# A gated convolution and MLP kernel on one core: one convolution over all tokens, or two causal halves with the second beside the first half's MLP

## The chip, the core and the metric

The kernel runs on one core of one Trainium2 chip. The core has a matrix engine (PE, with PEld for its weight loads), a vector engine (DVE), an activation engine (ACT), a small general engine (POOL) and a queue engine (SP) that issues most DMA transfers. PE writes into PSUM, eight banks of 512 f32 values per partition; only DVE and ACT read PSUM here. The metric is device time in microseconds; lower is better.

## What is computed

Two layers, each with a mixer A and an MLP B, on x of 2048 tokens and 512 channels. The reference, cut to what matters:

```
def _A_ref(q, k, v, shift_k, ssm_k, ssm_D):
    k_shift = sum of 4 taps of k along the tokens, per channel
    kv = k_shift * v
    y = causal convolution of kv with ssm_k (2048 taps per channel, by FFT of length 2 * S)
    y = y + kv * ssm_D
    return q * y

def _B_ref(x, w1, b1, w2, b2):
    h = gelu(layernorm(x) @ w1 + b1)          # 512 -> 1376
    return h @ w2 + b2                        # 1376 -> 512

x = A_q
x = x + _A_ref(_layernorm(x), A_k, A_v, ...)
x = x + _B_ref(_layernorm(x), ...)
x = x + _A_ref(_layernorm(x), A_k, A_v, ...)
x = x + _B_ref(_layernorm(x), ...)
```

The inner branch of A depends only on k, v and the filters, so y is the same in both layers and is computed once. It has no dependence on x: the convolution must be there before the first product with q, and nothing else.

## The kernel before

Everything is bf16 in one SBUF tensor (`ar`), with f32 statistics in `sm` and one PSUM tensor (`ps`). The program first records operations with their reads and writes (`P.op`), then orders them, then adds waits, then emits one instruction stream per engine. An engine executes its stream in order.

**The convolution** is a transform over half-integer frequencies of length 4096, done by matmuls. A token is t = 16 b + a, with b on the 128 partitions.
- `turn`-like code (L749) transposes the filter on PE into that layout; the result is evicted by L664 or L663 (the helper `evac`: DVE copies with `tensor_copy`, ACT with `activation`, either may take it).
- `stage1` (L757, matmul at L766): 64 columns of data as weights, 128 columns of cosines or sines; real and imaginary parts go to the two halves of the PSUM partitions. 256 matmuls for the filter, 256 for kv.
- `stage2` (L772, L779) for the filter, with 128 columns, and the same in `products` (L861, L872) for kv, with 64 columns. The weights are a 4 MB table that SP loads in 16 pieces.
- `products` multiplies by the filter's transform with two operands at once (L658 through the helper `tt`, 128x2048): the filter's transform R_H and a copy R_HS with real and imaginary partitions exchanged. The copy is made by 16 SBUF-to-SBUF DMAs of 256 KB.
- `inverse1` (L884, L896), 256 matmuls of 128 columns, and `inverse2` (L938, L953), 64 matmuls of 256 columns.
All of it is done in two channel parts, `PARTS`.

**The shift filter** (4 taps): two of four channel blocks of 128 go through PE (`shift_pe`, L802: transposes at L810, matmuls with diagonal tap matrices at L827, the product with v at L834), two on DVE (`shift_tt`, L837: seven operations of 128x2048 and one product per block, L658).

**The MLP part** is a loop over two layers and blocks of tokens (16 token tiles of 128): `BLOCKS0 = (1,1,2,2,2,2,2,2,2)` and `BLOCKS1 = (4,4,4,4)`. Per block: statistics on DVE (L985, L987), reciprocal root on POOL (L991, L993), normalisation on DVE (L1000), x += norm * y (two L658), statistics and normalisation again, a transposition (PE at L1047 for the first two tiles, a DMA on SP for the others), m1 (L1060: 44 matmuls with the block's tokens as columns), gelu on ACT (L1065), m2 (L1093: 11 matmuls of 512 columns per token tile; the last tile in three pieces at L1082), and the residual sum on DVE (L1097).

**The order** comes from a list scheduler in `schedule`: each operation has a cost, a priority (its path to the end plus table entries in BIAS and PB), an earliest time (HOLD), and PSUM banks from pools. DMAs are issued in program order on SP. In that order all of the convolution stands ahead of the MLP, which begins when `inverse2` has delivered its first token tiles.

Of the kernel before, what the change touches and what calls it, by code (L numbers as in the profile page):

```python
# [22 lines left out]
class Pool:  # L23


    def __init__(self, nb, cap, gate=False):
        self.nb, self.cap, self.used, self.gate = nb, cap, 0, gate


class Tile:  # L30


    def __init__(self, pool):
        self.pool = pool
        self.base = None
        self.left = 0
        self.ops = []


class Op:  # L40
    __slots__ = ("i", "engs", "eng", "fn", "dur", "preds", "succ", "prio", "tile", "dma", "start", "end",
                 "pos", "inc", "waits", "val", "npred", "ready", "bytes", "base", "extra", "gate", "tag", "allow")


class Prog:
# [6 lines left out]
    BIAS = {'': 1044190, 'fir0': 816272, 'fir1': 594035, 'fir2': 1000293455, 'fir3': 475782, 'h1': 868926, 'h2': 42492, 'ht': 880650, 'i1_0': 1240071, 'i1_64':  # L52
# [6 lines left out]
    SHY = {'fir0': 1021, 'fir1': 277, 'h1': 55, 'h2': 0, 'ht': 0, 'i1_0': 0, 'i1_64': 365, 'i2_0': 61, 'i2_64': 0, 'x1_0': 0, 'x1_1': 8, 'x1_2': 1351, 'x1_3':  # L59
        1268, 'x2_0': 0, 'x2_64': 462, 'z0': 261, 'z1': 833}  # L60
    PB = {0: 150814, 1: -52106, 2: -225577, 3: -123331, 4: 999221868, 9: 1276405, 44: 1379512, 45: 1434690, 47: 506509, 49: 453148, 51: 999588645, 52:
# [131 lines left out]
    def __init__(self, nc):  # L193
        self.nc = nc
        self.ops = []
        self.state = {}
        self.nodes = [(-1, None)]
        self.cache = {}
        self.tag = ""


    def _cells(self, ap):
# [59 lines left out]
    def op(self, eng, fn, dur, reads=(), writes=(), tile=None, dma=None, prio=0.0, nbytes=0, gate=()):  # L262
# [11 lines left out]
        for t in o.tile:  # L274
            for p in t.ops:
                preds.add((p.i, "psum"))
            t.ops.append(o)
            t.left += 1
# [14 lines left out]
    def _place(self, tiles, s):  # L293

        got, taken = [], set()
        for t in tiles:
# [4 lines left out]
            for b in range(0, 8, pool.nb):  # L301
# [4 lines left out]
                if best is None or k < best:  # L306
                    best = k
# [826 lines left out]
```

## Time and profile before

| what | value |
|---|---|
| median of 3 runs | 242.58 us (241.78 to 242.68) |
| span of the profiled execution | 239.8 us |
| what lies around the span, by the median | 2.8 us |
| PE busy / share / instructions | 226.5 us, 94%, 2310 |
| DVE | 175.7 us, 73%, 363 |
| ACT | 142.9 us, 60%, 223 |
| POOL | 34.8 us, 15%, 75 |
| DMA | 27.40 MB, mean 114 GB/s |
| granted PE clock, mean | 1.000 |
| first L1060 matmul (m1), last L1082 matmul (m2) | 84.2 us, 237.5 us |

The span runs from the first to the last instruction of the profiled execution; the page has no total time for that execution, so its span is compared with the median of the runs, which also holds the launch and the end. A matmul's duration on the page contains its latency, so that neighbours overlap and the sum of durations is more than the time in which PE was occupied. Prices per instruction are therefore better taken from runs of like instructions in the timeline or the chain: the run's length by its count. "Idle before" is the time an engine had nothing, with the event that ended it.

### The profile page before, as it was taken

What the parts mean: (1) busy time and instruction counts of PE and PEld (TensorE: products, weight loads), DVE (VectorE), ACT (ScalarE), POOL (GpSimd) and SP (SyncE); (2) the same over time, 40 slices, a digit from 0 to 9 for tenths busy, and PEclk for the clock granted to TensorE, in tenths of its full rate; (3) what the DMA queues carried; (4) which work ended last, traced back from release to release, by engine and by line L of the source; (5) the groups of instructions that cost most, each with busy time, mean ns of one, the idle gap of its engine ahead of it and who ended that gap; (6) DMA issues with size and microseconds to landing.
All of it is one profiled execution on the core that took longest, in us unless ns stands there. A gap on an engine that the chain in (4) does not pass through costs nothing.

```text
span 239.8 us, 5559 instructions
## 1 busy us (share of the span) xinstructions
PE 226.5 (94%) x2310; PEld 151.5 (63%) x2330; DVE 175.7 (73%) x363; ACT 142.9 (60%) x223; POOL 34.8 (15%) x75
## 2 busy tenths in 40 slices
PE   7988899886899999999999999999999999999996
PEld 3876777775899885777767665754444444444453
DVE  0779999999997989989999996978997401211214
ACT  3697999999998994665556253464532552436200
POOL 3250000000012222223141032022130100000000
PEclk9999999999999999999999999999999999999999
DMA  6999999999910004222020203313022203210022
GB/s 231 338 387 385 384 235 272 249 282 337 375 63 0 3 0 48 45 44 48 0 44 5 42 1 68 66 23 68 0 44 44 87 3 69 62 44 0 3 98 77
DMA packets 37035, 27.40 MB, mean 114 GB/s; under 512 B 19506, under 2 KB 29969, under 8 KB 37010
## 3 DMA queue, kind: packets, MB, share of 16 engines
q1 hardware_dynamic: 36446, 26.91, 38.1%
q8 instruction: 18, 0.29, 0.5%
q10 hardware_dynamic: 564, 0.14, 0.4%
q14 instruction: 7, 0.06, 0.1%
HBM read 16.82 MB, written 2.10 MB: 79 GB/s over the span
## 4 chain that ended last, share of the span: by engine, by line
PE 71%; DVE 15%; DMA 4%; ACT 4%; SPq 3%; issue 2%; DVEq 0%
PE ps L1060 32%; PE ps L1093 30%; DVE ar L658 8%; PE ps L896 5%; DMA ar<-in_A_v_dram 4%; ACT ar L663 4%; DVE ar L664 4%; SPq L647 3%; DVE ar L834 2%; PE ps L1082 1%; PE ps L872 1%; DVE sm L985 1%; PE ps L953 1%; DVE ar L1000 0%; PE ps L766 0%
## 5 line engine op out<-in xcount | busy, mean ns | idle before, releaser
L1065 ACT ACTIVATE ar<-ps,sm 128x256 bf16<-128x256 f32 (+5 forms) x143 | 67.8, 522 | 72.8 <-PE ps L1060 70.1
L1060 PE MATMUL ps<-ar 128*128 128x256 bf16 (+5 forms) x568 | 83.7, 296 | 0.2
L1093 PE MATMUL ps<-ar 128*128 128x512 bf16 (+1 forms) x329 | 78.9, 379 | 0.7
L663 ACT ACTIVATE ar<-ps 128x1024 bf16<-128x1024 f32 (+2 forms) x79 | 73.9, 1055 | 8.0 <-PE ps L766 3.2
L1060 PEld LDWEIGHTS ps<-ar 128*128 128x128 bf16 (+1 forms) x572 | 53.2, 100 | 29.4 <-ACT ar L1065 0.4
L658 DVE TENSOR_TENSOR ar<-ar 128x512 bf16<-128x512 bf16 (+3 forms) x108 | 63.8, 628 | 1.8 <-DMA ar<-in_A_k_dram 1.4
L1093 PEld LDWEIGHTS ps<-ar 128*128 128x128 bf16 (+1 forms) x341 | 33.2, 98 | 34.5
L1097 DVE TENSOR_TENSOR ar<-ar,ps 128x512 bf16<-128x512 bf16 x31 | 20.8, 682 | 43.2 <-PE ps L1093 43.1
L985 DVE BATCH_NORM_STATS2 sm<-ar 128x6 f32<-128x512 bf16 (+1 forms) x68 | 42.6, 650 | 0.3
L1000 DVE TENSOR_SCALAR ar<-ar,sm 128x512 bf16<-128x512 bf16 x64 | 24.1, 401 | 6.6 <-POOL sm L993 6.3
L993 POOL TENSOR_TENSOR sm<-sm 128x2 f32<-128x2 f32 (+2 forms) x26 | 20.5, 787 | 2.2
L766 PE MATMUL ps<-ar 128*64 128x128 bf16 x512 | 17.6, 221 | 3.0 <-DVE ar L664 1.0
L991 POOL TENSOR_SCALAR sm<-sm 128x2 f32<-128x2 f32 (+2 forms) x26 | 5.9, 226 | 95.9 <-DVE sm L987 95.7
L766 PEld LDWEIGHTS ps<-ar 128*64 128x64 bf16 x512 | 14.9, 110 | 5.4 <-DVE ar L664 1.3
L664 DVE CAST ar<-ps 128x1024 bf16<-128x1024 f32 (+1 forms) x15 | 17.5, 1181 | 0.4 <-PE ps L872 0.2
L896 PE MATMUL ps<-ar 128*128 128x128 bf16 x256 | 15.1, 220 | 1.0 <-DVE ar L658 0.5
L896 PEld LDWEIGHTS ps<-ar 128*128 128x128 bf16 x256 | 14.5, 114 | 1.4 <-ACT ar L663 0.8
L872 PE MATMUL ps<-ar 128*128 128x64 bf16 x256 | 9.6, 193 | 2.3 <-ACT ar L663 2.1
L664 DVE COPY ar<-ps 128x2048 bf16<-128x2048 bf16 (+1 forms) x6 | 5.7, 954 | 7.6 <-PE ps L749 7.4
L987 DVE BATCH_NORM_AGGREGATE sm<-sm 128x2 f32<-128x6 f32 (+1 forms) x64 | 10.8, 177 | 0.6
L872 PEld LDWEIGHTS ps<-ar 128*128 128x128 bf16 x256 | 8.2, 98 | 3.5 <-ACT ar L663 3.4
L779 PE MATMUL ps<-ar 128*128 128x128 bf16 x128 | 8.7, 220 | 0.9 <-ACT ar L663 0.8
(33 smaller groups left out, 72.0 us busy)
## 6 DMA issues: line engine op xcount, KB each, us to landing
ar<-tab_s SPq DMA_DIRECT2D x16, 256.0 KB, 10.0
ar<-ar SPq DMA_DIRECT2D x16, 256.0 KB, 4.6
ar<-in_A_ssm_k_dram SPq DMA_DIRECT2D x4, 512.0 KB, 5.5
ar<-in_A_k_dram SPq DMA_DIRECT2D x8, 256.0 KB, 7.7
ar<-in_A_v_dram SPq DMA_DIRECT2D x8, 256.0 KB, 9.7
ar<-in_A_q_dram SPq DMA_DIRECT2D x4, 512.0 KB, 7.8
out_dram<-ar SPq DMA_DIRECT2D x7, 256.0 KB, 2.0
ar<-in_B_w_dram SPq DMA_DIRECT2D x1, 1376.0 KB, 12.0
```

What stands on the lines that cost most here:

```text
L658: return P.op(eng, lambda e: e.tensor_tensor(o, a, b, op), dur, reads=[a, b] + list(more), writes=[o])
L663: return e.activation(dst, src(), AF.Copy)
L664: return e.tensor_copy(dst, src())
L766: r = e.matmul(Q(tl, 64 * ri, 64, i * 128, [1, 128]), w, m, start=True, stop=True)
L896: r = e.matmul(Q(tl, 0, 128, i * 128, [1, 128]), w, m, start=q == 0, stop=q == 1)
L985: P.op(DVE, lambda e, sj=sj, x=x: e.bn_stats(sj, x), 40.0 + 1.1 * w, reads=[x], writes=[sj], gate=gate)
L993: P.op(POOL, lambda e: e.tensor_tensor(r, v, hf, ALU.pow), 430.0 + 150.0 * n, reads=[v, hf], writes=[r])
L1000: P.op(DVE, lambda e: e.tensor_scalar(o, x, m, r, ALU.subtract, ALU.mult), 335.0, reads=[x, m, r], writes=[o])
L1060: r = e.matmul(Q(tl, 0, rows, 0, [1, w]), a, m, start=dk == 0, stop=dk == 3)
L1065: P.op(ACT, lambda e, dst=dst, tl=tl, rows=rows, bias=bias, w=w: e.activation(dst, Q(tl, 0, rows, 0, [1, w]), AF.Gelu_apprx_tanh, bias=bia ...
L1093: r = e.matmul(Q(tl, 0, 128, 0, [1, 512]), ins[fc][0], ins[fc][1], start=fc == 0, stop=fc == 10)
L1097: P.op(DVE, lambda e, x=x, tl=tl: e.tensor_tensor(x, x, Q(tl, 0, 128, 0, [1, 512]), ALU.add), 640.0, reads=[x], writes=[x], tile=tl)
```

## The change

The convolution is cut into two causal halves of 1024 tokens. With h0 and h1 the halves of the filter and X0 and X1 the transforms of the halves of kv, a transform of length 1024 over half-integer frequencies gives the lower half of a product as its real part and the upper half as its imaginary part. So the first half of y is the real part of H0 X0, and the second half is the real part of H0 X1 + (H1 - i H0) X0. Only the even frequencies of the former transform are needed (`k1 = 2 * arange`), and a token is now t = 8 b + a within a half.

- Stage 1 and stage 2 are done for h0, kv0, h1 and kv1. Stage 2 has 16 matmuls of 64 columns per tile, in all four cases, and writes its output in PSUM in groups of 4 columns.
- For the second half, `h2_1` forms H1 - i H0 as it leaves PSUM (16 `scalar_tensor_tensor` on DVE), a second set of eight swap DMAs exchanges its partitions, `p2` multiplies with X0 (8 operations of 2048), and `x2_1` has a product and a sum (8 of each) before the second `inverse1`.
- `inverse2` has 32 matmuls of 512 columns.
- The shift filter of all four channel blocks runs on PE, per half, with matmuls of 64 rows that use the two halves of the partitions and write to two banks. Keys of the first half are transposed on PE, those of the second by eight DMA transposes on SP.
- The first half's MLP (both layers, `BLOCKS` (1,1,2,2,2) and (2,2,2,2)) is interleaved with the second half's convolution; the second half's MLP, with blocks of 4, follows.
- The normalisation may run on DVE or ACT; for ACT, POOL computes minus mean times scale (two more operations per block).
- The list scheduler is gone. `arrange` takes a written order of all 1200 operations (SEQ), a letter for the engine of each operation that has a choice (ENGS) and a PSUM bank for each tile (BANKS).

The diff, cut to its core:

```
-    k1 = np.arange(128)[None, :]
+    k1 = 2 * np.arange(128)[None, :]
...
-PE_CH, PO_CH = (0, 1), ()
-PARTS = ((0, 64), (64, 64))
-BLOCKS0, BLOCKS1 = (1,1,2,2,2,2,2,2,2), (4, 4, 4, 4)
+BLOCKS = ((1, 1, 2, 2, 2), (2, 2, 2, 2)), ((4, 4), (4, 4))
...
+    def stage2(G, t):
+        tl = Tile(2)
+        ins = [(i, A(0, 128, R_S2 + (16 * t + i) * 128, [1, 128]), A(0, 128, G + (16 * t + i) * 8, [1024, 8], [1, 8])) for i in range(16)]
         def f(e):
             for i, w, m in ins:
-                r = e.matmul(Q(tl, 0, 128, i * n, [1, n]), w, m, start=True, stop=True)
+                r = e.matmul(Q(tl, 0, 128, i // 8 * 512 + i % 8 * 4, [32, 16], [1, 4]), w, m, start=True, stop=True)
             return r
...
+    def shift(half, c, K, V):
...
+        for a in (0, 4, -3, -2, -1, 1, 2, 3, 5, 6, 7):
+            lo, hi = max(a, 0), min(a + 4, 8)
+            for r in range(2):
+                ins.append((r, lo, hi - lo, A(64 * r, 64, kt + a % 8 * 144 + (16 if a >= 0 else 15), [1, 128]),
+                            A(64 * r, 64, R_DG + 256 * c + 64 * (lo - a), [1, 64 * (hi - lo)])))
...
+    P.tag = "x2_0"
+    for t in range(8):
+        tl = stage2(R_3, t)
...
+        for g in range(2):
+            tt(hap(R_1, t, R_2 - R_1, g), A(0, 128, HX + 1024 * t + 512 * g, [0, 2], [64, 8], [1, 64]), hap(HH, t, HI - HH, g), ALU.mult, 603.0)
...
+    P.tag = "h2_1"
+    for t in range(8):
+        tl = stage2(R_G1, t)
+        for g in range(2):
...
+                return e.scalar_tensor_tensor(o, x, SG, Q(tl, 0, 128, 512 * g, [1, 512]), ALU.mult, ALU.add)
+            P.op(DVE, f, 603.0, reads=[x, SG], writes=[o], tile=tl)
+    swap(R_3, R_HS1)
+    P.tag = "p2"
...
+        tt(o, A(0, 128, HX + 1024 * t, [0, 2], [64, 16], [1, 64]), o, ALU.mult, 1137.0)
...
+        tt(o, A(0, 128, xo, [0, 2], [64, 16], [1, 64]), o, ALU.mult, 1137.0)
+        P.tag = "sum"
+        tt(o, o, p, ALU.add, 1137.0)
+    P.tag = "i1_1"
+    inverse1(HH, HI, R_Z1)
...
+        def f(e):
+            if e is nc.scalar:
+                return e.activation(o, x, AF.Identity, bias=u, scale=r)
+            return e.tensor_scalar(o, x, m, r, ALU.subtract, ALU.mult)
+        P.op(BOTH, f, {DVE: 323.0, ACT: 705.0}, reads=[x, m, r, u], writes=[o])
...
-    P.schedule()
+    P.arrange()
```

PE's new order, by the parts named above: the first half's convolution up to `inverse2` with the second half's filter transform between its pieces; then the first half's MLP blocks, with `h2_1`, the second half's shift filter, stages 1 and 2, `inverse1` and `inverse2` between them; then the second half's MLP.

More of the change, by code (lines that the diff above doesn't have):

```diff
@@ L40 @@
 class Op:
[L41 to L42 removed]
+    __slots__ = ("i", "engs", "eng", "fn", "dur", "preds", "tile", "dma", "end", "pos", "inc", "waits", "val", "bytes", "tag")
 class Prog:
@@ L284, in op @@
                 o.preds[p] = "raw" if k in ("raw", "waw") else (k if p not in o.preds else o.preds[p])
-        o.gate = gate
-        o.eng = None
-        o.start = o.end = None
+        if self.first and ACT in o.engs:
+            o.preds.setdefault(self.first.i, "psum")
+        o.eng = o.end = None
         o.inc = False
@@ new lines, in arrange @@
+    def arrange(self):
+        self.order = {e: [] for e in (PE, ACT, DVE, POOL, SP)}
+        self.seq = [self.ops[i] for i in self.SEQ]
+        choice = iter(self.ENGS)
+        for o in self.ops:
+            o.eng = o.engs[0] if len(o.engs) == 1 else {"a": ACT, "v": DVE, "p": POOL}[next(choice)]
+        for t, b in zip(self.tiles, self.BANKS):
+            t.base = int(b)
+        last = [()] * 8
+        free = dict.fromkeys(self.order, 0.0)
+        for o in self.seq:
+            for t in o.tile:
+                if t.left == len(t.ops):
+                    for b in range(t.base, t.base + t.nb):
+                        for p in last[b]:
@@ L424, in sync @@
+            o.end = free[o.eng] + (2300.0 + o.bytes / 385.0 if o.dma else self.LAT)
+            o.pos = len(self.order[o.eng])
+            self.order[o.eng].append(o)
     def sync(self):
         known = {e: {} for e in self.order}
-        seq = sorted(self.ops, key=lambda o: (o.start, o.i))
-        bypos = {e: 0 for e in self.order}
-        heads = []
         ptr = {e: 0 for e in self.order}
@@ L697, in bass_interleave_layers__ssm_conv_h3__mixer_channel_mlp__prompt_kernel @@
-    for step in LOADS:
-        load(step)
-    for i in range(NPE):
-        z = A(0, 128, R_KT[i], [130, 16], [1, 2])
-        P.op(POOL, lambda e, z=z: e.memset(z, 0.0), 300.0, writes=[z])
-    tload(t_sm, row, 384, R_U, 256)
-    dconv = Pool(2, 4, True)
-    def warm(pool, n, w, dur, gate=()):
-        tl = Tile(pool)
-        z = A(0, 128, R_W, [1, w])
-        def f(e):
-            for i in range(n):
-                r = e.matmul(Q(tl, 0, 128, 0, [1, w]), z[:, :128], z, start=True, stop=True)
-            return r
-        P.op(PE, f, n * dur, reads=[z], tile=tl, prio=-1e9, gate=gate)
@@ new lines, in load_t @@
+    def load_t(x, half, o, w):
+        for a in range(0, 8, w):
+            dma(A(0, 128, o + 512 * a, [1, 512 * w]), dr(x, 512 * (1024 * half + a), [8 * 512, 128], [1, 512 * w]), w << 17)
+    load_h(0, R_1)
+    load_t(A_k, 0, R_8, 2)
+    load_t(A_v, 0, R_8 + 4096, 2)
+    for i in range(16):
+        tload(t_s2, 128 * 128, i * 1024, R_S2 + i * 1024, 1024)
+    tload(t_sm, row, 464, R_U, 256)
+    z = A(0, 128, R_W, [1, 512])
+    P.op(POOL, lambda e, z=z: e.memset(z, 0.0), 530.0, writes=[z])
@@ new lines, in bass_interleave_layers__ssm_conv_h3__mixer_channel_mlp__prompt_kernel, with f @@
+    P.tag = "warm"
+    tl = Tile(2)
+    def f(e, tl=tl, z=z):
+        for i in range(6):
+            r = e.matmul(Q(tl, 0, 128, 0, [1, 512]), z[:, :128], z, start=True, stop=True)
+        return r
+    P.op(PE, f, 2576.0, reads=[z], tile=tl)
+    P.tag = "taps"
+    for i in range(4):
+        o, t = A(0, 128, R_DG + i * 256, [64, 4], [1, 64]), A(0, 128, R_TC + 4 * i, [1, 4], [0, 64])
+        idn = A(0, 128, R_ID + 128, [0, 4], [1, 64])
+        P.op(POOL, lambda e, o=o, t=t, idn=idn: e.tensor_tensor(o, idn, t, ALU.mult), 613.0, reads=[idn, t], writes=[o])
@@ L960, in bass_interleave_layers__ssm_conv_h3__mixer_channel_mlp__prompt_kernel @@
-    for d0, n in PARTS:
-        P.tag = "i2_%d" % d0
-        inverse2(d0, n)
-    P.tag = "warm"
-    done = [o for o in P.ops if o.tag[:3] == "i2_" and o.engs == (PE,)]
-    ptr, pm1, pm2 = Pool(1, 2), Pool(1, 3), Pool(1, 3)
-    for i in range(NWARM):
-        warm(pm2, 4, 128, 56.0, done)
+    SG = M(0, 128, M_SG, [1, 1])
+    sg = A(0, 128, R_SG, [1, 1])
+    P.op(POOL, lambda e: e.tensor_copy(SG, sg), 190.0, reads=[sg], writes=[SG])
+    P.tag = "i1_0"
+    inverse1(R_1, R_2, R_3)
+    P.tag = "i2_0"
```

813 lines of the change are left out of this document (312 added, 501 removed), and 179 rows, old and new, of tables (BIAS, HOLD, PB, SEQ).

## The prediction

> **What bounds the kernel now.** I first read the page's 40 slices and then the chain of work that ended last.
>
> ```profile
> PE   7988899886899999999999999999999999999996
> DVE  0779999999997989989999996978997401211214
> ACT  3697999999998994665556253464532552436200
> DMA  6999999999910004222020203313022203210022
> GB/s 231 338 387 385 384 235 272 249 282 337 375 63 0 3 0 48 45 44 48 0 44 5 42 1 68 66 23 68 0 44 44 87 3 69 62 44 0 3 98 77
> ```
>
> A slice is 6 us. The DMA engines are full in slices 2 to 11, DVE in slices 4 to 12, and PE from slice 12 on. PE's row overstates the early slices, since its spans overlap and hide short waits. The chain gives the parts:
>
> ```profile
> 9.82 9.67 DMA ar<-in_A_v_dram
> ...
> 33.90 3.40 DVE ar L658 x3
> ...
> 68.63 8.21 PE ps L896 x144
> ...
> 145.75 5.41 PE ps L1093 x25
> ...
> 187.29 6.91 PE ps L1060 x32
> ```
>
> Columns: start, us, what. A load ends last up to 19.5 us, DVE up to about 52, ACT and PE in turn up to 77, DVE again up to 83. From the first L1060 matmul at 84.2 to the last L1082 matmul at 237.5, the chain is PE without a gap over 0.1 us. So the MLP is a block of 153 us at PE's full pace: 5.41/25 = 0.216 us for 512 columns, 3.50/32 = 0.109 for 256. The chain's L896 run gives 57 ns for 128 columns. The timeline gives two smaller prices:
>
> ```profile
> 17.85 1.37 PEld L766 LDWEIGHTS ps<-ar 128*64 128x64 bf16 x48
> 48.28 2.02 PEld L872 LDWEIGHTS ps<-ar 128*128 128x128 bf16 x64
> 50.23 18.25 DVE L658 TENSOR_TENSOR ar<-ar 128x2048 bf16<-128x2048 bf16 x16
> 52.62 20.27 ACT L663 ACTIVATE ar<-ps 128x1024 bf16<-128x1024 f32 x22 [0.23 <-DVE ar L658]
> ```
>
> Issue to issue, a stage-1 matmul takes 28.5 ns (two half-width ones share the array: 128 columns cost half of 57), a 64-column one 31.6, a 2048-element product 1.14 us on DVE, a 1024-element eviction 0.92 on ACT. The chain's L664 runs (2.26/2) give 1.13 for it on DVE.
>
> At these prices PE's work before is 2.7 us of warm-up matmuls, 65.7 of convolution, 152 of MLP. Within 237.5 us that leaves **17 us of idle PE**, all ahead of the MLP. About 5 of it is the wait for the first data. No rearrangement can win more than the other 12.
>
> **The change, part by part.** *PE's work stays the same.* 512 stage-1 matmuls, 96 transposes of filter and keys, 256 inverse-1 matmuls and the MLP's shapes (88 matmuls of 128 columns, 308 of 256, 176 and 352 of 512) are as before. Stage 2 goes from 128 x 57 + 256 x 31.6 ns = 15.4 us to 512 of 64 columns, 15.7 to 16.2. Inverse 2 is 32 x 0.216 instead of 64 x 0.109. The shift filter goes from four tiles of 4096 columns (1.78 us by L827) to eight that each have 22 matmuls of half height (K = 64) and again 4096 columns. If the two heights run at once, as the half widths do, that is 0.89 each, the same 7.1. Sum: 221 us with the warm-up.
>
> *DVE.* Removed: the shift of two channel blocks, 2 x (7 x 1.14 + 1.24) = 18.4 us. Added: 8 products and 8 sums of 2048 elements for the second half (18.2), and 16 scalar-tensor-tensor operations that replace evictions either engine could do. No row shows these; 0.34 (L658, 512 elements in SBUF) and 0.68 (L1097's duration, one operand in PSUM) bound them. I take 0.60, L1097's pace, as they also read PSUM: 9.7. DVE as a whole gains little. ACT gets 38 of the 64 normalisations; nearest rows are 0.59 (L1065's pace at 512) and 0.69 (its duration), so I take 0.7. POOL gets two more small operations per block (0.22 by L991), some 0.4 us of latency each time.
>
> *What moves* is the start of the MLP. I sum three stretches from the written order.
>
> **A, to the first MLP matmul.** SP's queue has 8.2 MB ahead of the last piece of the stage-2 table: half of h, k and v, 0.5 of q, the table, a quarter of the second half of h. The GB/s row gives 3.4 MB by 12 us, then 0.385 MB per us: 24.5 us. Then come 0.8 MB of filter (2 us), the eight swaps of 256 KB (2.1 MB at the 250 GB/s of the slices from 30 to 48, 8.4 us), 0.8 MB between them (2.2) and 1.5 to land: 38.6. Four products of 0.6 wait for the last swap: 41.0. Inverse 1 is 8 x 0.91 plus the last eviction: 49.3. From there to the first m1: 0.43 PE, 0.5 eviction, 0.7 for y, 0.7 statistics, 1.3 on POOL, 0.3 normalisation, 0.2 transposes, 0.5 eviction and some 0.15 at each handover, 5.7. The trace had 7.5 between the same points (76.67 to 84.18). **A = 55**, against 84.2. PE has done 43.7 us by then, DVE 43 and ACT 42, so none of them sets it.
>
> **B, from there to inverse 1 of the second half.** PE's order holds 54.8 us of MLP, 8 tiles each of stage 1 and of both stage 2s, and four shift tiles: **68.7**. DVE's order up to the last sum, which that inverse needs, holds 41.5 of convolution (9.7 + 4.5 + 9.1 + 9.1 + 9.1) and 27 of MLP (19 statistics of 0.60, 20 aggregations of 0.10, 5 norms of 0.32, 23 y operations of 0.34, 7 residual adds of 0.60): **68.5**. ACT has 55. Two engines are full at once, and each waits in order for the other.
>
> **C, the rest:** inverse 1 (7.3), inverse 2 (3.5), 97.7 of MLP: **108.4**. DVE has 59 here, and the second half's first block has 27.7 us of PE work over it for a chain of some 23. After the last matmul 2.3, as now.
>
> A + B + C + 2.3 = 234.4. For B's handovers I put a loss between 0 (at 110 to 140 us of the trace DVE was 9.9 busy of 10 and the chain on PE had no gap) and 10% of DVE's 68.5. I take 2.5, near the lower end, since that row has the same mix of MLP work at the same load. Span 236.9 against 239.8. The median of the runs is 242.58, so 2.8 lies around the span: **239.7 us**.
>
> [...] The trace has no matmul of half height, only half width at half the price. [...]
>
> PE's longest idle in the trace was 1.6 us, at the start, and the granted clock is 1.00 in every window. Yet the six warm-up matmuls of 512 columns come 0.43 us apart, twice the 0.216 of later, so the array starts at half pace. In A, PE has 27 us of work between 5.5 and 41 us; its 8 us of idle collects before inverse 1, which waits for the swaps. If it is one gap and the pace falls back, inverse 1 starts slow. At the start of the trace the slow pace lasted from 1.56 to at least 4.3 us (the warm-ups) and at most 8.8 (28.5 ns matmuls), 2.7 to 7.2 us, of which half is lost: 1.4 to 3.6. [...]
>
> **Rivals.**
> 1. *Everything packs.* The products start per channel half as swaps land, and DVE's fillers (first statistics of q) keep A near the 48.5 us that DVE's own 43 allow from its start at 5.5. Then 51 + 177.1 + 0.5 + 2.3 + 2.8 = **233.7**. For it: every engine has 42 to 44 us before the first m1. Against: the swap chain.
> 2. *DVE becomes the bound in B*, on the slower side. Its 68.5 us contain waits for swaps, POOL's longer chains and PE's residual tiles, and PE stands behind the last sum in its fixed order. At a density of 90% DVE needs 76, 7.5 more than PE's work: 234.4 + 7.5 + 2.8 = **244.7**. It decides from a loss of 5.4 us (density 92.6%). Against it: DVE ran from 20 to 68 us of the trace without a gap, though with little that had to come from PE's MLP.
> 3. *The clock falls in A* (PE idle in one gap before inverse 1): 239.7 + 1.4 to 3.6, middle **242.2**. For it: the slow start. Against it: the second half's filter stages can fill the gap, and ACT's evictions, as long as inverse 1's tiles, hide a part.
> 4. *The new PE shapes cost more than their rows.* Serial half heights: four tiles in B at 1.78, +3.5; stage 2 with scattered writes at up to 57 ns, +6.5 in B. Middle: **245**. In A, PE's idle hides most of it.
> 5. *The overlap doesn't come about,* if a late W2 or key transpose blocks SP's queue: B's first m2 is due at 60, W2 is issued at about 46 and took 14.6 to land in the trace, so it would cost up to 2. It is within the range.
>
> **Chances.** Forecast 0.45 (own range 236.5 to 242), rival 1 0.20, rival 2 0.20, rival 3 0.07, rival 4 0.08. A difference under 0.5% cannot be told from none here: 241.4 to 243.8. Faster: 0.39 + 0.20 + 0.02 = 0.61. Within: 0.06 + 0.06 + 0.04 + 0.02 = 0.18. Slower: 0.14 + 0.01 + 0.06 = 0.21. From 235 to 246 leaves out most of rival 1 and the tails of 2 and 4.
>
> **What would show it.** Step A: the first m1 matmul between 52 and 58 us; the last swap lands at 37 to 40; inverse 1 released by DVE's product. Step B: inverse 1 of the second half starts at 122 to 128, and who releases it (DVE's sum: rival 2). PE's idle in B: under 4 us, or 6 and more. Shift tiles: 0.9 or 1.8 us. Clock: matmuls of inverse 1 at 57 ns or 107. C: 108 to 110 with no gap. I am wrong if A ends after 60 or if DVE has waits of more than 5 us in B.

## The result and the profile after

The changed kernel takes 243.60 us (median of 17 executions, 242.52 to 247.07), the kernel before 241.89 (17, 240.99 to 242.68). The ratio is 1.0083, with a 95% interval of 1.0060 to 1.0105: 0.8% slower, where 239.7 and faster were predicted. The profiled execution has a span of 241.8 us and took 243.58. The ratios given here and below leave out executions that lie more than 1.5% above the same kernel's shortest one (that of e3 does not); the medians don't.

The granted PE clock of the changed kernel is 1.000 in 7 of the 17 executions (mean time 243.0), 0.993 in 9 (mean 244.6) and 0.986 in one (247.07). The profiled execution is one of the seven. In all 77 executions of the kernel before that were run beside the experiments below, the clock is 1.000.

The slices of the changed kernel's page (6.05 us each):

```profile
PE   7897697998899999899999999999999999999995
DVE  1697699999989999999999989385368486723004
ACT  2396699999879457998787976667429425541630
DMA  7999789759977990200620011600500050043002
GB/s 185 344 396 386 257 190 271 271 158 180 244 119 113 232 182 3 43 4 3 193 68 3 4 22 22 90 0 0 130 3 1 0 143 33 0 87 130 0 3 87
```

DVE has at least 8 tenths in every slice from 6 to 25; before, it had them in 4 to 12 and in 14 to 24. The second half's convolution now lies beside the MLP. The DMA engines are less than full in slices 5, 6, 8 and 9, where they were full before. The chain of waits of the same kernel (start, us, what):

```profile
27.22 2.23 issue
...
42.54 7.39 PE ps L616 x128
49.95 3.35 ACT ar L460 x4
...
61.18 3.22 ACT ar L835 x12
...
130.76 7.15 PE ps L616 x128
```

Inverse 1 of the first half starts at 42.5, that of the second half at 130.7. An "issue" of 2.23 us is new (the longest on PE before was 0.59): PE had all that the profile knows of and did nothing. The busy time by the stretches A, B and C of the prediction (us, then PE, PEld, DVE, ACT, POOL busy with counts, clock, DMA share, GB/s):

```profile
0.00:16.00 16.00, 13.67 (x214) 10.99 (x216) 8.77 (x16) 7.13 (x8) 4.50 (x18) 1.00 0.89 297
16.00:31.00 15.00, 11.21 (x317) 9.99 (x312) 10.68 (x13) 10.50 (x11) 1.13 (x4) 1.00 0.93 329
...
57.86:130.60 72.74, 70.07 (x867) 52.10 (x867) 70.73 (x119) 56.86 (x115) 23.00 (x48) 1.00 0.53 107
130.60:239.20 108.60, 108.57 (x654) 57.92 (x652) 63.14 (x149) 58.66 (x95) 16.59 (x42) 1.00 0.16 39
```

| stretch | predicted | measured | difference |
|---|---|---|---|
| A, to the first m1 matmul | 55 | 57.9 | +2.9 |
| B, to the second half's inverse 1 | 71.2 | 72.7 | +1.5 |
| C | 108.4 | 108.6 | +0.2 |
| end | 2.3 | 2.6 | +0.3 |
| around the span | 2.8 | 1.8 | -1.0 |

The table is the whole difference of 3.9 us in the profiled execution. C, a stretch of pure PE work, was right. So the questions are A, B and the clock. The span's surroundings were sized from the median of three runs; a single execution's time less its own span is 1.7 to 1.9 for both kernels. By good luck this hides 1.0 us of the miss: the span is 241.8 where 236.9 was predicted.

### The profile page after: what moved, and what is told of

It is laid out like the page before. It is cut to its first block, busy times and chain, and to the rows that moved or that the text cites. A ratio compares the mean times of both kernels' runs of the same rounds, so it can differ in the third digit from the quotient of the medians.

```text
span 241.8 us, 6074 instructions
## 1 busy us (share of the span) xinstructions
PE 228.0 (94%) x2544; PEld 151.7 (63%) x2544; DVE 179.6 (74%) x343; ACT 159.0 (66%) x255; POOL 57.3 (24%) x133
## 4 chain that ended last, share of the span: by engine, by line
PE 66%; DVE 21%; issue 3%; DMA 3%; ACT 3%; POOL 2%; SPq 0%; DVEq 0%; POOLq 0%
PE ps L864 24%; PE ps L830 23%; DVE ar L455 9%; PE ps L616 6%; DVE sm L748 4%; PE ps L535 4%; DVE ar L703 3%; PE ps L547 3%; DMA ar<-in_A_ssm_k_dram 2%; PE ps L592 2%; PE ps L518 1%; DVE ar L598 1%; PE ps L634 1%; DVE ar L868 1%; ACT ar L460 1%
## 5 line engine op out<-in xcount | busy, mean ns | idle before, releaser
L830 PE MATMUL ps<-ar 128*128 128x256 bf16 (+4 forms) x572 | 82.2, 297 | 1.6 <-ACT ar L460 1.1
L460 ACT ACTIVATE ar<-ps 128x1024 bf16<-128x1024 f32 (+3 forms) x73 | 68.4, 1022 | 13.2 <-PE ps L535 9.5
L455 DVE TENSOR_TENSOR ar<-ar 128x512 bf16<-128x512 bf16 (+3 forms) x108 | 63.9, 629 | 1.8 <-ACT ar L460 0.6
L748 DVE BATCH_NORM_STATS2 sm<-ar 128x6 f32<-128x512 bf16 x64 | 43.1, 684 | 0.6
L766 ACT ACTIVATE ar<-ar,sm 128x512 bf16<-128x512 bf16 x38 | 29.4, 813 | 7.2 <-POOL sm L758 7.2
L535 PE MATMUL ps<-ar 128*64 128x128 bf16 x512 | 18.0, 227 | 4.2 <-issue 3.5
L535 PEld LDWEIGHTS ps<-ar 128*64 128x64 bf16 x512 | 15.6, 114 | 6.7 <-issue 4.5
L547 PE MATMUL ps<-ar 128*128 128x64 bf16 x512 | 18.8, 193 | 0.3
L461 DVE CAST ar<-ps 128x1024 bf16<-128x1024 f32 (+1 forms) x13 | 14.4, 1137 | 5.8 <-PE ps L535 3.3
L547 PEld LDWEIGHTS ps<-ar 128*128 128x128 bf16 x512 | 16.9, 98 | 2.9 <-ACT ar L460 1.2
L767 DVE TENSOR_SCALAR ar<-ar,sm 128x512 bf16<-128x512 bf16 x26 | 10.5, 415 | 7.8 <-POOL sm L758 7.7
L616 PE MATMUL ps<-ar 128*128 128x128 bf16 x256 | 14.7, 219 | 0.6 <-DVE ar L455 0.6
L616 PEld LDWEIGHTS ps<-ar 128*128 128x128 bf16 x256 | 14.5, 114 | 0.8 <-DVE ar L455 0.8
L703 DVE SCALAR_TENSOR_TENSOR ar<-ar,sm,ps 128x512 bf16<-128x512 bf16 x16 | 11.2, 741 | 0.7 <-PE ps L547 0.7
```

Of the source, the lines that this page charges most:

```text
L455: return P.op(eng, lambda e: e.tensor_tensor(o, a, b, op), dur, reads=[a, b] + list(more), writes=[o])
L460: return e.activation(dst, src(), AF.Copy)
L535: r = e.matmul(Q(tl, 64 * ri, 64, i * 128, [1, 128]), w, m, start=True, stop=True)
L547: r = e.matmul(Q(tl, 0, 128, i // 8 * 512 + i % 8 * 4, [32, 16], [1, 4]), w, m, start=True, stop=True)
L616: r = e.matmul(Q(tl, 0, 128, i * 128, [1, 128]), w, m, start=n == 0, stop=n == 1)
L748: P.op(DVE, lambda e, sj=sj, x=x: e.bn_stats(sj, x), 600.0, reads=[x], writes=[sj])
```

## The experiments

Three readings of A and B stood against each other. *Theory:* in A PE waits for its own instructions, which come by DMA behind the loads. *Rival 1:* the loads themselves, or the order of SP's queue, bound A. *Rival 2:* DVE is the bound in B. The kernels of one group ran on one chip, beside the kernel before (241.7 to 242.0 in each group).

### What PE stands for in A

PE's timeline in the changed kernel, where no engine is named as the releaser:

```profile
15.34 1.16 PE L592 MATMUL ps<-ar 64*128 64x256 bf16 x23
16.79 1.93 PE L592 MATMUL ps<-ar 64*128 64x256 bf16 x43 [0.29 <-issue]
...
20.68 1.03 PE L535 MATMUL ps<-ar 128*64 128x128 bf16 x30
22.98 0.25 PE L535 MATMUL ps<-ar 128*64 128x128 bf16 x2 [1.27 <-issue]
...
26.25 0.97 PE L535 MATMUL ps<-ar 128*64 128x128 bf16 x28
```

The third stop, of 2.23 us, follows the last line. Between two stops lie 126 or 127 matmuls, each with a weight load: about 254 instructions. The page's DMA part has a queue of its own for instructions, with 20 packets of 16 KB in the whole kernel:

```profile
q8 instruction: 20, 0.33, 0.6%
```

In the trace these packets run at 14.4, 20.5 and 27.0 us, each for 1.0 to 1.1 us, and PE resumes 1.4 us after each has ended (16.79, 22.98, 29.45). Counting from the moment PE resumed, the next packet begins 3.7 and 4.0 us later while the DMA engines are full, and 2.4 later at 31.8, after a stretch in which they were not (a DMA share of 1.07 and 1.01 over the two waits, of 1.01 over the third, but of 0.54 from 28.00 to 29.45). (The trace doesn't show when a block is asked for; that it is when PE resumes is assumed here.) So a block of instructions takes 3.7 + 1.1 + 1.4 = 6.2 us, then 4.0 + 1.1 + 1.4 = 6.5, and PE uses one up in 4.9 us (16.79 to 21.70), then in 4.2 (22.98 to 27.22). The differences, 1.3 and 2.2 us, are the stops.

DVE's timeline shows where the stops go. After the first loads, its two longest waits in A end with matmuls that come after a stop. It never waits for a swap: from 37.6 us its products run without a gap to 46.1, and inverse 1 starts in the middle of them.

```profile
23.83 3.49 DVE L461 CAST ar<-ps 128x1024 bf16<-128x1024 f32 x3 [1.40 <-PE ps L547]
...
29.79 2.36 DVE L461 CAST ar<-ps 128x1024 bf16<-128x1024 f32 x2 [2.38 <-PE ps L535]
...
37.58 8.51 DVE L455 TENSOR_TENSOR ar<-ar 128x1024 bf16<-128x1024 bf16 x14
```

**c_changed_again** is the changed kernel unaltered, beside e5, e6 and e7.

> The changed kernel as it is, on the chip of the next three. Its first 60 us should show the three stretches in which PE is released by nothing that the profile names (0.3, 1.3 and 2.2 us at 16, 22 and 27 us). Theory (a PE that idles for over 2 us in A is put to half pace): in some executions the clock's mean is 0.993 and the time 1 to 2 us longer than in those at 1.000. Rival (the clock has nothing to do with it): no such link. Time 242.5 to 245.

It took 244.35 (243.66 to 247.01), ratio 1.0136 (1.0064 to 1.0208). The stops are 0.49, 1.08 and 2.23 us, the first m1 comes at 58.1. All four executions have a clock of 0.993 or less, so the link to the time could not be seen inside this group.

**e7_code_shifted** moves the program by 32 matmuls:

```
-        for i in range(6):
+        for i in range(2):
             r = e.matmul(Q(tl, 0, 128, 0, [1, 512]), z[:, :128], z, start=True, stop=True)
+        for i in range(36):
+            r = e.matmul(Q(tl, 0, 128, 0, [1, 64]), z[:, :128], z[:, :64], start=True, stop=True)
```

> Four of the six warm-up matmuls of 512 columns are replaced by 36 of 64 columns, so that the rest of PE's program lies 32 matmuls (with their weight loads) further on. Nothing else changes. Theory (PE stands at the end of each 16 KB of its program, every 127 matmuls or so): all three stretches without a releaser come 32 matmuls earlier in the order of the work: the one after 28 of the 32 L535 matmuls comes at the end of the L547 run before it, the one after 30 of 32 comes before those 32. Rival (a wait for data that the profile does not name): they stay where they are in the order, after 30 and 28 matmuls of L535. Time within 1.5 us of the changed kernel's.

Its PE timeline:

```profile
14.74 0.44 PE L537 MATMUL ps<-ar 128*64 128x128 bf16 x9 [0.69 <-issue]
...
19.02 1.03 PE L594 MATMUL ps<-ar 64*128 64x256 bf16 x20
21.08 0.20 PE L594 MATMUL ps<-ar 64*128 64x64 bf16 x2 [1.03 <-issue]
...
24.45 0.99 PE L549 MATMUL ps<-ar 128*128 128x64 bf16 x28
27.29 0.29 PE L549 MATMUL ps<-ar 128*128 128x64 bf16 x4 [1.85 <-issue]
```

L537, L594 and L549 are L535, L592 and L547 of the changed kernel. All three stops are 32 matmuls earlier in the order of the work: after 28 of the L547 run that precedes the old place, after 20 of 22 shift matmuls, and 9 + 23 matmuls ahead of the first old place. A wait for data would have stayed. What PE stands for is its own program. The single time, 248.35 at a clock of 0.979, missed the expectation. Its trace has a clock of 0.59 and 0.56 from 28 to 32 us, right after the stop, but the first m1 comes at 58.3, only 0.4 later than in the changed kernel. Most of the excess lies in B, which lasts 77.1 us: PE waited 3.41 us ahead of the first m2, and the ten m2 matmuls after that took 4.47 us instead of 2.32.

A block's end cost up to 2.23 us in this kernel, where matmuls of 28 to 33 ns meet full DMA engines (a DMA share of 1.05 or more in each window of 2 us from 20 to 26 us). The kernel before has "issue" waits too (0.59, 0.40 and 0.16 us; the first comes 1.5 us after a 16 KB packet has ended). Its PE work is less dense: 125 matmuls from 20 to 30 us, where the changed kernel has 196 in spite of its stops.

### Fewer loads ahead of the requests

Each of SP's first 33 loads waits until the k-th before it has landed:

```
+        big = [o for o in self.seq if o.dma and o.eng == SP and o.fresh][:33]
+        for a, b in zip(big, big[k:]):
+            b.preds.setdefault(a.i, "raw")
```

> Edit: each of SP's first 33 loads waits until the fourth load ahead of it has landed, so that never more than four are outstanding; nothing else changes. Theory 1 (the first stretch is late because PE's own stream stalls, marked issue, 1.27 us at 21.7 and 2.23 us at 27.2, while loads fill the DMA engines, and this delays stage 2 of the filter, the swaps and the products): the two stalls together fall from 3.5 us to under 1.5, the first m1 matmul moves from 57.9 us to 55.5 to 57, time 1 to 2 us less. Rival (the landing of the stage-2 table sets the stretch, the stalls only fill a wait that is there anyway): stalls may shrink, but the first m1 stays at 57.5 to 59, time unchanged or up to 1 us more.

> Each of SP's first 33 loads waits until the seventh before it has landed, so that a request for PE's instructions finds less ahead of it in the DMA engines. Theory (these 16 KB requests wait behind the loads): the stretches without a releaser fall from 3.8 us to under 1, the first m1 matmul comes at 55.5 to 56.5 instead of 57.9, no half-pace stretch, time 240.5 to 242. Rival (the loads themselves bound A): PE's waits turn into waits for the table and the filter, first m1 at 58 or later, time 243.5 or more, as with a pace of four.

> As with seven, with ten loads outstanding. Theory: the stretches without a releaser are between those of the changed kernel and of a pace of seven, 1 to 3 us; time 241.5 to 243.5. Rival (the loads bound A): the same as the changed kernel within 0.5 us.

| | stops in A, us | inverse 1 starts | first m1 | time | ratio |
|---|---|---|---|---|---|
| changed kernel, beside e5 and e6 | 3.8 | 42.8 | 58.1 | 244.35 | 1.0136 (1.0064 to 1.0208) |
| k = 4 (e1) | none | 45.6 | 62.5 | 249.44 | 1.0325 (1.0280 to 1.0371) |
| k = 7 (e5) | 1.2 | 39.2 | 56.7 | 243.23 | 1.0064 (1.0042 to 1.0085) |
| k = 10 (e6) | 2.0 | 41.8 | 58.6 | 243.71 | 1.0078 (1.0057 to 1.0099) |

Counted as stops here and below are the "issue" waits at a block's end, each of which ends 1.3 to 1.6 us after a 16 KB packet has ended. Not counted are waits of 0.43 and 0.40 us that e5 and e6 have at 10.5 us, ahead of the first such packet, and of 0.60 and 0.77 us at about 18 us, ahead of their first stage-2 matmul, where the trace with k = 4 names the table.

In these traces fewer loads in front go with shorter stops, in order of k, and with k = 7 inverse 1 starts 3.5 us earlier. None of the three reached the time that its theory expected. With k = 4 the table comes too late: PE waits 1.4, 1.4 and 2.1 us for it, the rival's mechanism, though it costs more than the rival allowed. But e5's m1 gains 1.4 us of those 3.5, not all. Its PE timeline shows where the rest went:

```profile
39.22 3.76 PE L621 MATMUL ps<-ar 128*128 128x128 bf16 x64 [0.60 <-DVE ar L460]
45.03 3.77 PE L621 MATMUL ps<-ar 128*128 128x128 bf16 x64 [2.05 <-DVE ar L460]
```

and DVE's own timeline in the same kernel names what DVE waited for:

```profile
42.47 2.50 DVE L460 TENSOR_TENSOR ar<-ar 128x1024 bf16<-128x1024 bf16 x4 [2.11 <-DMA ar<-ar]
```

Inverse 1's second half waits for products, and those for the last swap, which stood on SP behind two tables and a load of q. So both theory and rival 1 hold, one after the other: once the stops shrink, SP's order is late next.

k alone doesn't set the stops: later kernels with k = 7 have 1.0 us (e12), 2.3 (e16) and 3.0 (e10), in one trace each. The start of inverse 1 goes with the stops and not with k. It is 39.2 and 39.3 with stops of 1.2 and 1.0 us (e5, e12), 40.4 to 41.8 with 1.4 to 2.3 (e17, e6, e16), and 41.4 to 42.8 with 2.5 to 3.8 (e10 with k = 7, e11 with k = 6, and without pacing e2, e3, e4, e7, e8, e14 and the changed kernel). Left out are e1 and e9, which wait for a table, and e13 and e15, which change PE's order in A.

### The order of SP's queue

The edits, cut to what differs, move entries of the written order: each pair is an operation and the one that it goes ahead of. 94 and 93 are the last two swaps, 191 and 192 the pieces of T2, 428 is a product of the second token tile.

```
 e8, e9     +        for a, b in ((94, 191), (93, 191)):
 e10, e11   +        for a, b in ((94, 191), (93, 191), (428, 429)):
            +            seq.remove(a)
            +            seq.insert(seq.index(b), a)
```

e9 and e10 also have the pacing with k = 7, e11 with k = 6; e10 and e11 have the edit of e3 (below) as well.

> On SP the last two swaps of the first half go ahead of 0.3 MB of tables and 0.5 MB of q, which stood before them. Loads are not paced. Theory (A is set by PE's code requests, so that the swaps are late from the start; their tail matters only after that): products are limited by DVE here, so under 0.5 us is gained, 243.5 to 244.5. Rival (the queue ahead of the last swaps sets inverse 1): its start moves by 1 us or more, time 242 to 243.

> A pace of seven and the swaps first together. With the pace alone DVE's products waited 2.1 us for the last swap, and inverse 1 2.05 us for those. Theory: both waits go, the first m1 matmul comes at 54.7 to 55.2 instead of 56.7, B and C stay at 72.9 and 108.6, time 241 to 241.6. Rival (the next thing in A is as late: evictions on ACT or the y chain): m1 at 56 or later, time 242.5 to 243.

> As the run before, and a normalisation on DVE no longer waits for the POOL operation that only ACT's form needs, and a product of the second token tile no longer stands ahead of the first tile's statistics on DVE. Theory: the way from the end of inverse 1 to the first m1 is 0.5 to 0.8 us shorter, time 240.3 to 241. Rival (that way is set by ACT's evictions): no gain, 241 to 241.6.

> As the run before with six loads outstanding instead of seven. Theory: PE's stretches without a releaser shrink from 2.2 to about 1.5 us, but the loads come a little later; time within 0.5 us of the run before. Rival (the loads are now the bound): 1 us slower or more.

e8 (no pacing) took 243.39, ratio 1.0061 (1.0043 to 1.0078): inverse 1 at 42.3 and m1 at 57.7, 0.4 us better than in c_changed_again, as the theory had it. e9 took 243.78, 1.0050 (1.0021 to 1.0078), and missed. With the swaps ahead, the small table U behind them is what came late:

```profile
41.69 8.93 PE L625 MATMUL ps<-ar 128*128 128x128 bf16 x128 [2.25 <-DMA ar<-tab_small]
```

The 128 matmuls take 8.93 us instead of 7.38, since part of them ran at half pace after that wait (the clock is 0.50 from 42 to 45 us). e10 took 242.68, 1.0022 (0.9997 to 1.0048): from the start of inverse 1 to the first m1 it has 15.11 us against 15.32 in the changed kernel and e8, a gain of 0.2 where 0.5 to 0.8 were expected. POOL's third operation is worth no more than that on this way. e11 took 243.38, 1.0067 (1.0045 to 1.0088), 0.7 slower than e10, with a stop of 1.8 us at a block further on.

### B: the sums, and W2

**e2_sums_left_out** cuts the eight sums of 2048 elements to 4 columns, so that the second half's y is not what the reference asks for; 8.6 us of DVE's work in B go.

```
-        tt(o, o, p, ALU.add, 1137.0)
+        o, p = [A(0, 128, r + 64 * t, [1, 4]) for r in (HH, R_3)]
+        tt(o, o, p, ALU.add, 70.0)
```

> Edit: the eight sums of 128x2048 ahead of the second inverse 1 are cut to 4 columns each; this leaves out the contribution of the first half's inputs to the second half of y, apart from those columns, and takes 8.6 us of work off DVE. Theory 2 (in the stretch from the first m1 to the second inverse 1 DVE is as full as PE, and PE stands for DVE): PE's idle there falls from about 3.4 us to under 1.5, and the time falls by 2 to 3 us. Rival (PE's idle there comes from ACT's queue and POOL's chains, and DVE has slack): under 1 us less.

It took 244.98, ratio 1.0104 (1.0054 to 1.0155). B lasts 72.9 us (59.1 to 132.0), no less than the 72.7 of the changed kernel. DVE used the time to run ahead, with 138 operations inside B instead of 119, and PE did not follow. The wait ahead of the first m2, of which more below, is 1.89 us here and 1.15 in the changed kernel; without it B is 71.0 against 71.6, so the sums are worth 0.6 us at most. DVE is busy for 70.7 of B's 72.7 us, and yet it is not the bound in B.

**e3_no_wait_for_shift** removes the wait of DVE's normalisations for the POOL operation that only ACT's form needs.

```
+            if o.eng == DVE and len(o.engs) == 2 and not o.tile and o.tag[0] in "qz":
+                del o.preds[max(p for p in o.preds if self.ops[p].eng == POOL)]
```

> Edit: normalisations on DVE no longer wait for POOL's two extra operations (minus mean times scale), which only ACT's normalisations use. Rival to theory 2 (POOL's chains, twice as long in operations and stretched while DVE multiplies, cost the time): DVE's 7.7 us of waits for L758 fall by half, time 0.7 to 2 us less. Theory 2: the waits shrink, but most stand where DVE has slack (after 140 us), and the time changes by less than 0.5 us.

247.31, 1.0257 (1.0186 to 1.0328); B is 73.1, so nothing is gained. The two executions at a clock of 0.993 took 245.10 and 245.84, the two at 0.986 248.78 and 249.26. What made it slower than the changed kernel by more than the clock stays open.

What then is lost in B? In the changed kernel's trace, matmuls in B start 56 ns apart with 128 columns, 109 with 256, 216 with 512, 29 in stage 2, 28 in stage 1 and 42.5 on average in the shift tiles. Times their counts (88, 240, 110, 208, 128, 88, and 0.25 for four transposes) that is 5.0 + 26.2 + 23.8 + 6.0 + 3.6 + 3.7 + 0.25 = 68.5 us: the 68.7 of the prediction. B took 72.7, so the loss is 4.2 where 2.5 were allowed. Its largest piece is the wait ahead of the first m2 (1.15 us in the profiled execution). The timeline names two more, 0.92 us for ACT at 101 and 0.38 for a transpose at 118; the other 1.8 lie in gaps too short for it to name. For the wait ahead of the first m2 the changed kernel's two traces name two releasers, first the profiled execution,

```profile
64.52 2.54 PE L864 MATMUL ps<-ar 128*128 128x512 bf16 x11 [1.15 <-ACT ar L835]
```

and then c_changed_again:

```profile
65.06 2.32 PE L864 MATMUL ps<-ar 128*128 128x512 bf16 x10 [1.46 <-DMA ar<-in_B_w_dram]
```

Both the gelus and W2 end there, within about a microsecond. The next group moves W2's loads (197, 196, 198) and U (32) forward; 274 is the first load of the second half's keys. All have the edits of e10, and e12 and e13 the pacing with k = 7. In e13 and e15 the second half's filter (loads 131 to 134, transposes 135 to 142) also goes behind the first four swaps and the last stage-2 tiles.

```
 e12 to e15 +        for a, b in ((32, 191), (94, 191), (93, 191), (428, 429), (197, 274), (196, 274), (198, 274)
 e13, e15   +            , (131, 183), (132, 183), (134, 183), (133, 183), (135, 153), (136, 153), (137, 153), (138, 153)
            +            , (141, 153), (142, 153), (139, 153), (140, 153)
```

> As with the short chain and a pace of seven, and on SP the small table U goes ahead of the last two swaps (inverse 1 had to wait 2.25 us for it once they stood first) and the three loads of W2 go ahead of the keys and transposes of the second half. Theory (B's excess is in part the first m2's wait, which has two causes, the gelus and W2): B shrinks from 72.9 to about 72.2, since the gelus still end 0.6 to 1.2 us late, and A ends at 55 to 57; time 240.5 to 242. Rival (W2 alone holds the first m2): B shrinks by 1.7 to 71.2.

> The run with W2 earlier without the pacing of the loads. Theory: the stretches without a releaser are back at 3.5 to 4 us in all, with half pace behind them in most executions; first m1 at 57 to 57.7, B as in the paced run, time 242 to 243. Rival (pacing does nothing once SP's order is right): within 0.4 us of the paced run.

> As the run before, and the 1 MB of the second half's filter is loaded after the first four swaps instead of before them; its transposes follow the last stage-2 tiles on PE. Theory (PE's requests for instructions wait behind the loads): the loads end 2.5 us earlier, so the longest stretch without a releaser, at 27 us, falls from 1.2 to 2.2 to under 0.8, and the clock stays at 1.000; first m1 at 54 to 56, time 240 to 241.5. Rival (the filter is then too late for PE's order): waits for it at 32 us, first m1 at 57 or later, time 242 or more.

> The run with the second half's filter later, without the pacing. Theory: between the paced run and the unpaced run with the filter early, 241 to 242.5, since at 27 us less load stands ahead of PE's request. Rival: a stretch of 2 us stays, time 242.5 or more.

e12's PE timeline:

```profile
52.71 1.02 PE L646 MATMUL ps<-ar 128*128 128x512 bf16 x4 [2.33 <-DMA ar<-tab_small]
...
56.67 0.84 PE L842 MATMUL ps<-ar 128*128 128x128 bf16 x12
...
61.91 2.32 PE L876 MATMUL ps<-ar 128*128 128x512 bf16 x10
...
127.93 7.31 PE L628 MATMUL ps<-ar 128*128 128x128 bf16 x128
```

The first m2 has no wait, and B is 71.3 us (56.67 to 127.93). It is 71.6, 71.5 and 71.4 in e14, e13 and e15, which have W2 early too, and 72.6 to 73.4 in eleven traces with W2 late (both of the changed kernel, e1 to e3, e5, e6 and e8 to e11). (e7 has W2 late too, and its 77.1 come from the wait and the half pace told above.) So W2's place on SP costs B about 1.4 us (72.7 less 71.3), as the rival of the expectation had it; the gelus, which the theory thought nearly as late, cost little. But W2 now stands ahead of the last piece of the table T2, and inverse 2 waits 2.33 us for that. e12 took 241.86, ratio 0.9996 (0.9975 to 1.0016): as fast as the kernel before. e14, the same without pacing, took 243.87, 1.0103 (1.0074 to 1.0131), with stops of 2.8 us (1.0 in e12) and inverse 1 at 42.4: between these two kernels the pacing is worth 2 us.

e13 and e15 took 246.18 and 245.00 (1.0163, 1.0138). The stop at 27 us was still 1.99 and 1.85 us long. The 1 MB was no longer in front at that time. If the request is made when the block before is begun, at about 21 to 22 us, the table's loads still filled the engines then (9 tenths from 18 to 24 us on e15's DMA row); that it is made then is not shown. And ahead of inverse 1 PE waited 1.98 us for DVE, and the first m1 came at 62.0 and 60.5: the filter was too late for PE's order, as e13's rival had it.

e16 (k = 7) and e17 (k = 8) are e12 with that piece ahead of W2 too:

```
+            , (192, 274), (197, 274), (196, 274), (198, 274)
```

> As with U and W2 earlier and a pace of seven, and the last piece of the inverse's table T2 goes ahead of W2, since inverse 2 had to wait 2.3 us for it. Theory (what the change lost stands in A's loads, in the order of SP's queue and in the first m2's wait for W2): inverse 2 runs without that wait, the first m1 comes at 54.3 to 55.2, B stays at 71.3, C at 108.5; the span is 237 to 238 and the time 239 to 240 in executions without a half-pace stretch, 1.5 to 4 us more in the others; median 239.5 to 241. Rival (W2, now later, holds the first m2 again): A ends at 54.5 but B is 72.5 or more, time 241 or more.

> The same with eight loads outstanding. Theory: a little more waits ahead of PE's requests, so the stretches without a releaser grow by up to 0.5 us and half-pace executions are more frequent; median 0 to 1 us above the run before. Rival (seven holds the table back): 0 to 0.5 us below it.

243.93 (241.17 to 245.45), ratio 1.0051 (1.0017 to 1.0084), and 243.95 (240.44 to 245.23), ratio 1.0005 (0.9969 to 1.0041). e16 missed the 239.5 to 241 that were expected, and e17 is level with e16, with stops of 1.4 us where more than e16's 2.3 were expected. The first m1 comes at 55.5 in both, the earliest of all, but B is 75.6 and 76.8. In both PE waits 2.60 us soon after the first m1; in e16:

```profile
59.47 5.82 PE L842 MATMUL ps<-ar 128*128 128x128 bf16 x72 [2.60 <-ACT ar L847]
```

and the timeline of POOL in e16 shows for whom:

```profile
58.18 1.08 POOL L695 CAST sm<-ar 128x10 f32<-128x10 bf16 x2 [2.61 <-DMA ar<-in_B_b_dram]
```

The gelu's bias, loaded behind W2, the keys and a DMA transpose, was the next thing to be late. Moving it as well wasn't tried. The clock of e16 is then 0.69 from 60 to 62 us and 0.50 from 62 to 64, and the 72 matmuls take 5.82 us instead of e12's 4.23. Without the wait and this loss of 1.6, e16's profiled execution (244.06) would be near 240 us, and e12's median without its 2.33 near 239.5; these are estimates, and no run shows them.

### No overlap

**e4_no_overlap** puts the whole convolution of both halves ahead of the MLP, all else as in the change.

```
-        self.seq = [self.ops[i] for i in self.SEQ]
+        cut = next(o.i for o in self.ops if o.tag == "q0")
+        self.seq = [self.ops[i] for i in self.SEQ if i < cut] + [self.ops[i] for i in self.SEQ if i >= cut]
```

> Edit: the same operations, engines and PSUM banks, but the whole convolution of both halves is ordered ahead of everything of the MLP. If the overlap is what the change lives from: the second half's convolution then needs DVE 41 us and ACT 28 for 25 us of PE, so the first m1 comes at 90 to 95 us and the time is 246 to 252 us. If DVE and ACT are so full in the overlap that nothing is won there: 242 to 245 us, as with the overlap.

307.34, ratio 1.2712 (1.2638 to 1.2787); both theories were far off. The first m1 comes at 138.1 instead of 57.9. The clock on e4's page and one stretch of its table by windows:

```profile
PEclk9999999975956558955999999999999999999999
```

```profile
100.00:110.00 10.00, 0.00 (x0) 0.00 (x0) 10.00 (x10) 0.57 (x1) 0.00 (x0) 0.50 0.15 59
```

For 10 us DVE forms products and sums while PE has nothing. The clock in these 10 us is 0.50, and PE's next 10 us have 0.66. Without MLP work beside it the second half's convolution takes 80 us in this order. So this written order needs its overlap. What overlap as such is worth is not shown: engines, PSUM banks and the places of the DMAs were all written for the interleaved order, PE waits 6.1 us for the transposes of the keys here and 13.5 for DVE, and the kernel before, which has no overlap either, takes 241.9. A version without overlap that has an order of its own was not run.

## Why the prediction was wrong, point by point

- **The price of PE's new shapes** was right: half heights run side by side, 0.94 us per shift tile (22 x 42.5 ns) against 0.89, where one after the other would be 1.78, and a stage-2 matmul takes 29 ns in B and 32.5 in A, where up to 31.6 were put down. Rival 4 falls.
- **A, start of inverse 1** (41.0 predicted, 42.5 measured) is the step whose mechanism failed. The sum had the queue of loads and the last swap as the bound, and put PE's stops at nothing. In the trace SP issues the swaps at 27.5, 33.3 and 37.1, behind evictions that wait for PE, and PE had stood still for 3.8 us. DVE never waits for a swap; its evictions waited 1.40 and 2.38 us for PE, and inverse 1 waits for its products. No term of the sum held this: I counted PE's work against the time it had and took the rest for slack. With the stops at 1.0 and 1.2 us (e12, e5) inverse 1 starts at 39.3 and 39.2, earlier than predicted. That the sum missed by no more than 1.5 us is luck.
- **A, from inverse 1 to the first m1:** 15.3 us in the changed kernel, 14.0 in the sum (8.3 and 5.7). From the first matmul of inverse 2, at 51.0, it is 8.5 and 6.8. The trace of before had 7.5 for what I put at 5.7, and that row was the better guide.
- **B's loss:** 4.2 instead of 2.5. Its place was given to DVE, which e2 acquits. 1.4 of it is W2, which rival 5 named (up to 2 us for a late W2) and the forecast left out of its sum; where the rest comes from is in part open.
- **The sign.** Measured against the 241.9 of the kernel before, the forecast of 239.7 was a gain of 2.2 us. The start of inverse 1 took 1.5 of it, the way to the first m1 1.3 and B 1.5. No one of the three alone turns it into a loss.
- **Rival 2** (DVE the bound in B, 244.7) gives nearly the measured time by a mechanism that isn't there.
- **Rival 3** (the clock falls in A, 242.2) is half there. Of the 17 executions after, 10 have a clock below 1.000, and the nine at 0.993 take 1.6 us more than the seven at 1.000. But the gap is not the one ahead of inverse 1, where PE waited 0.60 us. In c_changed_again (columns as in the table of windows above):

```profile
26.00:28.00 2.00, 0.44 (x16) 0.28 (x10) 0.63 (x2) 1.51 (x2) 0.00 (x0) 1.00 0.67 242
28.00:30.00 2.00, 1.33 (x42) 1.24 (x43) 0.99 (x1) 0.54 (x1) 0.00 (x0) 0.99 0.99 285
30.00:32.00 2.00, 2.00 (x36) 2.00 (x32) 1.75 (x3) 1.51 (x2) 0.00 (x0) 0.50 1.09 253
32.00:34.00 2.00, 2.00 (x46) 2.00 (x44) 0.98 (x2) 1.14 (x2) 0.00 (x0) 0.66 0.24 12
```

  PE stands from 26.4 to 28.7, and in the two rows from 30 to 34 the clock is 0.50 and 0.66. The same stop of 2.23 us in the profiled execution left it at 1.00. So one and the same stop goes with a fall of the clock in some executions only; what decides it is not shown.
- **Rival 1** (everything packs, 233.7) falls with A.
- **The range** of 235 to 246 holds 243.6, but that is luck: it was drawn so wide for rivals 2 and 4, whose mechanisms aren't there. The forecast's own range, 236.5 to 242, does not hold it, and the direction was wrong.

Most of A's excess (m1 at 55.5 in e16 and e17) and 1.4 us of B's are thus shown by runs that moved them. That all of it could be won back at once is not: each repair of SP's order made another load late, and no version was measurably faster than the kernel before.

## What to carry to other kernels

Where loads fill the DMA engines, look for "issue" stops about 127 matmuls (with their weight loads) apart. PE's program came through the same engines here (20 packets of 16 KB, 0.6% of the time of all 16); a block of it took 6.2 to 6.5 us, while 127 matmuls of 33 ns took 4.2. A block's end cost up to 2.2 us, and in some executions a stretch at half pace came after it (clock 0.50 from 30 to 32 us in c_changed_again). In a sum over a load queue that is full, put down for every transfer on it when it must land, the small ones too (a table, a bias), since a piece moved ahead made another one late here (waits of 2.25 us in e9, 2.33 in e12 and 2.60 in e16). And if a trace of before has a row for a whole way (7.5 us), take that row rather than a sum of its parts.

## What the runs showed that was not expected

- PE's 16 KB blocks in A take 1.0 to 1.1 us of transfer each, but under full loads they begin only 3.7 to 4.0 us after PE went on with the block before; PE goes on 1.4 us after their end.
- POOL's copy of 128x3 elements took 5.98 us (the median of its four is 0.2) beside DVE's products, which ended in the same moment (timeline of POOL, then of DVE, whose row holds the last eleven of the products shown above, in the changed kernel):

```profile
40.17 5.98 POOL L578 COPY ar<-ar 128x3 bf16<-128x3 bf16 x1 [4.50 <-PE ps L535]
```

```profile
39.38 6.71 DVE L455 TENSOR_TENSOR ar<-ar 128x1024 bf16<-128x1024 bf16 x11
```

  At 110 us POOL's two L758 operations took 1.2 us each (the median is 0.19), a part of the chain in B. They ran beside three L455 products of 128x2048 on DVE, which ended 0.1 us before them. What held POOL is not shown.
